# First two experts' second-layer weights split during the attention, by VectorE and GpSimd, with buffers refilled in order of release

## The chip, the cores and the metric

One NeuronCore of a Trainium2 chip. The metric is the device time of one execution in microseconds (us). The kernel before took 423.86 us (median of three runs, 423.17 to 424.08).

## The reference

Causal attention of 8 batches x 12 heads over 448 positions of 64 features feeds a mixture of experts with a capacity limit. Cut to what matters:

```python
scores = np.where(mask, -1e9, scale * np.matmul(q, k.transpose(0, 1, 3, 2)))
attn = softmax(scores)                       # 8 x 12 x 448 x 448
x = np.matmul(attn, v)  ->  (3584, 768)      # heads side by side
probs = softmax(x @ w_gate)                  # 8 experts
for e in range(8):
    tok = tokens whose best expert is e; the 80 of largest gate weight are kept
    h = np.maximum(x[tok] @ w1[e], 0.0)      # 768 -> 1024
    out[tok] = gate_w[tok, None] * (h @ w2[e])   # 1024 -> 768
```

All inputs and the output are float32. `w1[e]` is 768 x 1024 and `w2[e]` is 1024 x 768; the two take 6.3 MB for each expert and are read once.

## The kernel before

The kernel has two stages. In the attention (about the first 275 us) a loop runs over 48 pairs of heads, six pairs (`pr.p` 0 to 5) for each of the eight batches (`bt.b`). The work of one pair is laid out by hand in eight slots (`CYCLE`, slot number `k`), and every engine executes in the order in which it is written there. TensorE computes the scores `sp` (L376), VectorE masks and scales them (`ns`, `nb`, L386, operations `m0` to `m6`, one for each tile of 64 queries), ScalarE raises them (`prob`, L393, `e0` to `e6`), TensorE transposes the previous pair's probabilities (`tp`, L411), ScalarE copies them out of PSUM (`PT`, L419, `c0` and `c1`), TensorE multiplies by the values (`xp`, L440), and VectorE copies the result (`xu`, L446). GpSimd splits the queries and keys of the pair three places ahead into two float16 parts (`split_pair`, cast L333 and two subtractions L335). Between these, steps of the routing of the batch before stand at numbered slots (`STEPS`): gate products, the ranking of the tokens, and the rows `xr` (L646) that are written to the scratch tensor `xs`. On SyncE's queue the slots 1, 4 and 7 of a pair issue one part of a weight piece each (L214), and, where no piece is under way, a store of zeros to the output.

The weights are cut into 32 pieces of 128 x 3072 float32 (1.5 MB), in the order of `PIECES`: three chunks of 128 x 1024 for a first-layer piece, four chunks of 128 x 768 for a second-layer piece. Ten buffers hold them in strict rotation: seven in `wpool`, two in `wearly` (which the attention uses for queries and keys), one more that appears at its end. Seven pieces are loaded from pair 5 on; three more follow at the end of the attention; the 22 others come through L203 as buffers come free.

In the expert stage ScalarE casts each chunk, scaled by `SW` = 32, to float16 (`wh`, L1236), and VectorE computes what the cast lost (`wl`, L1221). There are 12 `wh` and 11 `wl` slots, which TensorE frees. A split chunk costs TensorE three float16 products in the first layer (L1305, L1307, L1308) or two in the second (L1301, one of which carries both parts of the hidden values, and L1303). The function `whole` names 21 of the 112 chunks that are not split: TensorE multiplies their float32 values directly (L1293). TensorE's order is by hand here (first layer of expert e, then second layer of expert e - 1); the others are placed by the compiler's scheduler. A buffer whose chunks are all split is free when the last `wl` of it is done; one with a whole chunk is free when TensorE has read it.

Of the kernel before, what the change touches and what calls it, by code (L numbers as in the profile page):

```python
# [7 lines left out]
F32 = mybir.dt.float32  # L8
F32R = mybir.dt.float32r
F16 = mybir.dt.float16  # L10
# [23 lines left out]
EARLY = {'gp0': 16, 'gs0': 18, 'gp1': 24, 'gs1': 26, 'lp': 32, 'lg': 34, 'logit': 37, 'shifted': 38, 'chosen': 40, 'sums': 40, 'one_hot': 41, 'weight': 41, 'weighted': 42, 'columns': 42, 'parts': 43, 'r0t': 45, 'r1t': 45, 'r0c': 46, 'r1c': 46, 'c3w': 48, 'rl': 49, 'c0w': 50, 'c3l': 51, 'c0l': 52, 'lt': 53, 'c2w': 54, 'c2l': 55, 'c1w': 56, 'c1l': 57, 'cp': 58, 'ro': 59, 'places': 60, 'places_more': 61, 'gt': 62, 'own': 63, 'earlier': 64, 'rank': 65, 'rr': 66, 'rr_more': 67, 'tn': 68, 'tab': 69, 'rp': 70, 'row': 71}  # L34
ROWS_EARLY = [(0, 0, 14, 1, 1), (0, 1, 22, 1, 4), (1, 0, 30, 1, 4), (1, 1, 47, 7, 8)]
LATE = 19

TAIL = """
rest3 ta ya rest3 v0 tb yb rest3 rest rest v1 rest2 turned vy guard invert rest placed w rest2 rest gp0 wy rest5 gp1 close piece gs
# [8 lines left out]
def attention_then_moe(  # L48
# [24 lines left out]
    assert NT == 4 and LAST == QB and D == NP * P and D // 2 <= S - LAST  # L73


    const = ctx.enter_context(tc.tile_pool(name="const", bufs=1))
    keep = ctx.enter_context(tc.tile_pool(name="keep", bufs=1))
    wpool = ctx.enter_context(tc.tile_pool(name="wraw", bufs=1))
# [98 lines left out]
    WBUF, WMORE = max(2, 8 - max(1, NSL)), 3  # L177

    WEARLY = 2

    RING, WHOLE = 3, 3
    qk_raw = wearly.tile([P, PW], F32, name="qk", tag="w", bufs=WEARLY)
    qk_parts = wearly.tile([P, 2 * PW], F16, name="qk16", tag="w", bufs=WEARLY)
    wload = []
    wmore = [wearly]

    def piece():

        e, which, c, k = PIECES[len(wload)]
        x = len(wload) % (WBUF + WMORE)  # L190
        pool, bufs = (wpool, WBUF) if x < WBUF else (wmore[0], WEARLY) if x < WBUF + WEARLY else (wmore[1], WMORE - WEARLY)
        t = pool.tile([P, k, PW // k], F32, name="wraw", tag="w", bufs=bufs)
        wload.append(t)
        return t, (w1 if which == 1 else w2)[e, :, c:c + k, :]

# [9 lines left out]
    def piece_parts():  # L205
# [8 lines left out]
            nc.sync.dma_start(t[:, j, x * half:(x + 1) * half], src[:, j, x * half:(x + 1) * half])  # L214
        return [lambda j=j, x=x: part(j, x) for j in range(k) for x in range(2)]


    mv = one_hots = mv_flat = oh_flat = expert_cols = tables = table_rows = None
    identb = before = dec = number = number_after = pnum = tbase = wgd = slots_e = slots_t = None
# [826 lines left out]
    with tc.manual_schedule():  # L1046
# [20 lines left out]
        for i, pr in enumerate(pairs):  # L1067
            bt = pr.bt
            if pr.p == 0:
                bt.xu = spool.tile([P, NP, S], F32, name="xu", tag="xu")  # L1070
                bt.sums = spool.tile([P, NP * TILES], F32, name="sums", tag="sums", bufs=3)
                if bt.b < B - 1:
                    batch_plan(bt)
            pr.xu, pr.sums = bt.xu, bt.sums
            if i and i % PH == 0:
                load_values(i // PH)
            products, masked, raised = scores_groups(pr, i)
            ops = {"s0": lambda: products(0), "s1": lambda: products(1)}
            for t in range(TILES):
                ops[f"m{t}"], ops[f"e{t}"] = lambda t=t: masked(t), lambda t=t: raised(t)  # L1080
            if i:
                for x, (work, copy) in enumerate(transpose_groups(pairs[i - 1], i < APART)):
                    ops[f"t{x}"], ops[f"c{x}"] = work, copy
            if i >= 2:
                values.append(values_group(pairs[i - 2]))
                ops["v"], ops["xu"] = values[-1]
            for k in range(SLOTS):
                for name in CYCLE[k].split():
                    if name in ops:
                        ops.pop(name)()  # L1090
                for f in plan.pop(i * SLOTS + k, []):
                    f()

                if i < WHOLE and k == 4:
                    load_pair(i + RING)
                if i >= WHOLE - 1 and k == (5 if i < WHOLE else 0) and i + RING + 1 < n:
                    load_pair(i + RING + 1)
                if k == 5 and pr.p == NP - 1 and i + 2 < n:
                    split_pair(i + 2)
                    split_pair(i + 3)  # L1100
                if k == 6 and pr.p < NP - 2 and WHOLE <= i + 3 < n:
                    if i >= 2:
                        nc.gpsimd.tensor_copy(tie, pairs[i - 2].xu[:, pairs[i - 2].p, 0:1])
                    split_pair(i + 3)

                if i == n - 2 and k == 0 and len(wload) >= WBUF and not parts:
                    load_piece()

                if i > 4 and k in (1, 4, 7):
                    if not parts and len(wload) < WBUF:  # L1110
                        parts = piece_parts()
                    if parts:
                        parts.pop(0)()
                    elif zdone[0] < N:
                        zero_rows()
        for f in parts:
            f()
        while len(wload) < WBUF:
            load_piece()
        while len(wload) < WBUF + WEARLY:  # L1120
# [76 lines left out]
    def whole(e, which, c):  # L1197

        if e >= E - 2:
            return e == E - 1 and which == 2 and c >= NC2 - 1  # L1200
        return c >= NC2 - 2 if which == 2 else c >= (NC1 // 2 if e == 0 else NC1 - 1)

    SW, SX = 32.0, 8.0
    NF = F // P
    HALF = NF // 2

# [6 lines left out]
    def split_pieces(m):  # L1213

        first = done[0]
        done[0] += m
        order, lows = [], []

        def low(l, src, h):
            with tc.issue_after((low_after or last_of)[-1].ins):  # L1220
                return nc.vector.scalar_tensor_tensor(out=l, in0=src, scalar=SW, in1=h, op0=ALU.mult, op1=ALU.subtract)  # L1221

        for i in range(first, first + m):
            while len(wload) <= i:
                load_piece()
            e, which, c, k = PIECES[i]
            for j in range(k):
                src = wload[i][:, j, :]
                order.append(c + j)
                if whole(e, which, c + j):  # L1230
                    parts_of[(e, which, c + j)] = (src,)
                    continue
                h = wsplit.tile([P, PW // k], F16, name="wh", tag="wh", bufs=HIS, padded_shape=[P, max(F, D)])
                l = wsplit.tile([P, PW // k], F16, name="wl", tag="wl", bufs=LOS, padded_shape=[P, max(F, D)])
                with tc.issue_after(batches[-1].raised.ins):
                    nc.scalar.activation(h, src, AF.Copy, scale=SW)  # L1236
                lows.append((l, lambda l=l, src=src, h=h: low(l, src, h)))
                parts_of[(e, which, c + j)] = (h, l)
        return order, lows

    def split_now(m):
        order, lows = split_pieces(m)
        for _, f in lows:
            f()
        return order
# [155 lines left out]
    for s in range(NSL):  # L1401
        if s:
            done[0] = 0
            wload.clear()
        units = []
        for e in range(E):
            u = Unit()
            u.e, u.s = e, s
            units.append(u)
        n1, n2 = NC1 // K1, NC2 // K2  # L1410
        prev = None
        g = gather(units[0])
        token_weights[s]()
        while s == 0 and len(wload) < WBUF + WMORE:
            load_piece(g)

        with tc.manual_schedule(engines={mybir.EngineType.PE}):
            for e in range(E + 1):
                if e < E:
                    u = units[e]  # L1420
                    if e == 0:

                        order, lows = split_pieces(n1)
                        u.order = order[NC1 // 2:] + order[:NC1 // 2]
                        units[1].order, more = split_pieces(n1)
                        for nx in units[1:AHEAD]:
                            gather(nx)
                        for _, f in lows:
                            low_after.append(f())
                        inputs(u)  # L1430
                        low_after.append(u.xl)
                        for _, f in more:
                            f()
                    elif e > 1:
                        u.order = split_now(n1)
                    if e + AHEAD < E:
                        gather(units[e + AHEAD])

                    def between(p=prev, nx=units[e + 1] if e + 1 < E else None):
                        if p and p.e:  # L1440
                            outputs(units[p.e - 1])
                        elif nx and not p:
                            inputs(nx)
                    if prev:
                        hidden(prev)
                    layer1(u, between)
                if prev:
                    prev.order = split_now(n2)
                    if e == E:
                        hidden(prev)  # L1450

                    between = None
                    if e + 1 < E:
                        between = lambda u=units[e + 1]: inputs(u)
                    elif e == E and prev.e:
                        between = lambda u=units[prev.e - 1]: outputs(u)
                    layer2(prev, between)
                    if e == E:
                        outputs(prev)
                prev = units[e] if e < E else None  # L1460
# [37 lines left out]
```

## Time and profile before

| | us |
|---|---|
| median of three runs | 423.86 |
| the profiled execution | 424.38 |
| its span, first to last instruction | 422.7 |
| TensorE busy | 399.8 (95%) |
| ScalarE busy | 370.7 (88%) |
| VectorE busy | 349.3 (83%) |
| GpSimd busy | 221.6 (52%) |
| DMA, mean over the span | 261 GB/s |

The shares are means over two stages with different limits, so the rows further on are taken by stretch. A matmul's duration on the page is that of a pipelined instruction; the pace of TensorE is read from the starts of the first instructions of successive groups. An idle time in brackets is that of the engine just before the row, with what ended it.

### The profile page before, as it was taken

The numbers are of one execution on the slowest core, as the hardware profiler recorded it, in microseconds if no ns is written. First come the engines' busy times: TensorE is split into PE (matmuls) and PEld (weight loads), VectorE is DVE, ScalarE is ACT, GpSimd is POOL, SyncE is SP. The second block draws the span as 40 slices with busy tenths as digits, with TensorE's granted clock in tenths as the row PEclk, the third lists the DMA queues.
The fourth block names the chain that finished last, engine by engine and source line by source line (L and its number), as shares of the span: only waits on it lengthen the run. The fifth ranks groups of instructions, "written<-read, shape, count | busy, mean of one in ns | idle before, by whom it ended". The sixth has DMA issues, their size and how long they took to land. (4 is left out here: it accounts for less than half of the span.)

```text
span 422.7 us, 19609 instructions
## 1 busy us (share of the span) xinstructions
PE 399.8 (95%) x7982; PEld 341.1 (81%) x7983; DVE 349.3 (83%) x1226; ACT 370.7 (88%) x980; POOL 221.6 (52%) x388
## 2 busy tenths in 40 slices
PE   5999999999999999999999999988999999999993
PEld 2688788787788878888878887875599999999993
DVE  3677688788978879888888897777789999998991
ACT  4999999999999999999999998874879898897790
POOL 3698546765845963865684586515511255230002
PEclk9999999999999999999999999999999999999998
DMA  6569977987898697798697443564489999999911
GB/s 204 155 208 323 293 266 222 339 272 241 268 329 262 223 304 251 243 272 288 204 288 259 150 145 118 206 197 190 117 302 395 380 417 396 390 422 426 383 35 47
DMA packets 42106, 110.18 MB, mean 261 GB/s; under 512 B 5234, under 2 KB 29554, under 8 KB 38816
## 3 DMA queue, kind: packets, MB, share of 16 engines
q1 hardware_dynamic: 40816, 105.20, 71.6%
q0 software_dynamic: 1056, 3.51, 2.6%
q8 instruction: 62, 1.02, 1.0%
q14 instruction: 28, 0.23, 0.2%
q10 hardware_dynamic: 144, 0.23, 0.2%
HBM read 85.35 MB, written 23.99 MB: 259 GB/s over the span
## 5 line engine op out<-in xcount | busy, mean ns | idle before, releaser
L393 ACT ACTIVATE prob<-ns,nb 128x448 f32<-128x448 f32 (+6 forms) x336 | 167.9, 503 | 15.3 <-DVE nb L386 14.5
L386 DVE CUSTOM_DVE_ANT_0 ns<-sp,mask 128x448 f32<-128x448 f32 (+6 forms) x336 | 124.9, 418 | 40.5 <-PE sp L376 33.5
L440 PE MATMUL xp<-PT,vt 128*64 128x128 f32 (+3 forms) x1536 | 95.8, 277 | 0.3 <-issue 0.3
L1221 DVE SCALAR_TENSOR_TENSOR wl<-wraw,wh 128x768 f16<-128x768 f32 (+1 forms) x91 | 92.1, 1077 | 3.0 <-ACT wh L1236 2.9
L335 POOL TENSOR_TENSOR qk<-qk,qk 128x448 f16<-128x448 f32 x90 | 91.9, 1043 | 3.6
L419 ACT COPY PT<-tp 128x1024 f32<-128x1024 f32 x89 | 89.0, 1000 | 3.0 <-PE tp L411 2.6
L440 PEld LDWEIGHTS xp<-PT,vt 128*64 128x64 f32 x1536 | 80.1, 137 | 13.7 <-issue 1.0
L376 PE MATMUL sp<-qk 64*64 64x384 f16 (+8 forms) x1974 | 79.2, 283 | 4.7 <-DMA qk<-k_t 4.7
L1236 ACT ACTIVATE wh<-wraw 128x768 f16<-128x768 f32 (+1 forms) x91 | 79.1, 932 | 3.5 <-PE hp L1308 1.5
L411 PE MATMUL tp<-ident,prob 64*128 64x64 f32 x1424 | 63.3, 227 | 6.0 <-ACT PT L419 4.2
L411 PEld LDWEIGHTS tp<-ident,prob 64*128 64x128 f32 x1424 | 51.9, 139 | 16.6 <-ACT PT L419 8.3
L393 ACT ACTIVATION_READ_ACCUMULATOR prob<-ns,nb 128x1 f32 x336 | 64.3, 191 | 0.0
L376 PEld LDWEIGHTS <-qk 64*64 64x64 f16 x1890 | 50.9, 106 | 12.7
L1394 POOL DMA_INDIRECT out<-yo,idx x8 | 19.7, 2466 | 66.0 <-ACT yo L1391 61.8
L333 POOL CAST qk<-qk 128x896 f16<-128x896 f32 x45 | 42.0, 933 | 8.5 <-DMA qk<-k_t 8.4
L1308 PEld LDWEIGHTS <-wl 128*128 128x128 f16 x362 | 36.1, 100 | 1.4 <-DVE wl L1221 1.2
L1305 PEld LDWEIGHTS <-wh 128*128 128x128 f16 x362 | 36.4, 101 | 0.9 <-issue 0.9
L1307 PEld LDWEIGHTS <-wh 128*128 128x128 f16 x362 | 36.2, 100 | 0.0
L1305 PE MATMUL hp<-xh,wh 128*128 128x80 f16 x320 | 35.3, 202 | 0.8 <-issue 0.8
L1308 PE MATMUL hp<-xh,wl 128*128 128x80 f16 x320 | 35.3, 202 | 0.0
L1307 PE MATMUL hp<-xl,wh 128*128 128x80 f16 x320 | 35.3, 202 | 0.0
L446 DVE COPY xu<-xp 128x448 f32<-128x448 f32 x48 | 29.7, 619 | 5.5 <-PE xp L440 5.1
(193 smaller groups left out, 633.1 us busy)
## 6 DMA issues: line engine op xcount, KB each, us to landing
wraw<-w SPq DMA_DIRECT2D x25, 1536.0 KB, 13.8
qk<-q_t SPq DMA_DIRECT2D x48, 224.0 KB, 3.9
out<-mask SPq DMA_DIRECT2D x56, 192.0 KB, 4.0
qk<-k_t SPq DMA_DIRECT2D x47, 224.0 KB, 4.3
vt<-v_t SPq DMA_DIRECT2D x16, 576.0 KB, 6.1
wraw<-w SPq DMA_DIRECT2D x30, 256.0 KB, 5.2
xs<-xr SPq DMA_DIRECT2D x18, 384.0 KB, 4.3
wraw<-w SPq DMA_DIRECT2D x16, 192.0 KB, 4.4
```

The lines of the kernel that those rows point to most:

```text
L335: nc.gpsimd.tensor_tensor(out=l[:, part], in0=x[:, part], in1=h[:, part], op=ALU.subtract)
L376: nc.tensor.matmul(pr.sp[t][to], q[rows, t * QB:(t + 1) * QB], k[rows, 0:WIDTH[t]], start=(x == 0), stop=(x == len(terms) - 1), skip_group ...
L386: nc.vector.tensor_tensor_reduce(out=ns[:, 0:w], in0=pr.sp[t], in1=mask[:, S - w:S], scale=-1.0 / 8.0, scalar=HUGE, op0=ALU.add, op1=ALU.m ...
L393: nc.scalar.activation(pr.P[:, OFF[t]:OFF[t] + w], ns[:, 0:w], AF.Exp, bias=nb, scale=-1.0, accum_out=pr.sums[:, pr.p * TILES + t:pr.p * T ...
L411: nc.tensor.transpose(tp[r][:, at:at + QB], pr.P[rows, off:off + P], ident[rows, rows])
L419: (nc.scalar.copy if how == "a" else nc.vector.tensor_copy)(pr.PT[:, g], pr.tp)
L440: nc.tensor.matmul(xp[rows, x0 * QB:x1 * QB], st["vt"][:, c, p * P + j * DH:p * P + (j + 1) * DH], pr.PT[:, g, 1 - j if crossed else j, at ...
L1221: return nc.vector.scalar_tensor_tensor(out=l, in0=src, scalar=SW, in1=h, op0=ALU.mult, op1=ALU.subtract)
L1236: nc.scalar.activation(h, src, AF.Copy, scale=SW)
L1305: nc.tensor.matmul(o, wh[:, ws], ah[:, c, :], start=(x == 0 and i % per == 0), stop=False, skip_group_check=True)
L1307: nc.tensor.matmul(o, wh[:, ws], al[:, c, :], start=False, stop=False, skip_group_check=True)
L1308: nc.tensor.matmul(o, wl[:, ws], ah[:, c, :], start=False, stop=(x == n - 1), skip_group_check=True)
```

## The change

Six things change. (1) The four second-layer pieces of experts 0 and 1 come first in `PIECES`. They are loaded during the attention into `w4`, `w5`, `w6` and `w4` again, at pairs fixed by `LOADS`. (2) Their 16 chunks are split during the attention: VectorE multiplies a chunk in place by 32 (16 instructions), GpSimd casts it to float16 (16) and subtracts the cast from it in two halves (32). The table `PRESPLIT` places them by pair and slot: one scaling each in slots (1, 7), (2, 7) and (4, 1), three casts in (4, 4), three subtractions each in (1, 3) and (2, 3); scalings and casts in batches 1 to 6, subtractions in batches 2 to 7. (3) The halves stay in four buffers, `w0` to `w3`, each of the size of a raw piece. (4) The other pieces go to buffers in the order of `FIRST` and `NEXT_USE` instead of the strict rotation. (5) `whole` names 13 chunks instead of 21: the two last second-layer chunks of experts 0 and 1 are among those split ahead, and the last first-layer chunk of experts 1 to 4 is split in the expert stage. (6) In that stage the second layers of experts 0 and 1 are neither cast nor subtracted any more.

```diff
+LOADS = [5, 7, 9, 25, 31, 37, 45]
+PRESPLIT = {(1, 3): (0, 0, 3), (1, 7): (1, 0, 0), (2, 3): (0, 0, 3), (2, 7): (1, 0, 0), (4, 1): (1, 0, 0), (4, 4): (0, 3, 0)}
...
+    PRE = 4 if WBUF == 7 and E > 1 and NC2 == 2 * K2 else 0
+    FIRST = [f"w{x}" for x in range(WBUF)] + ["e"] * WEARLY + ["m"] * (WMORE - WEARLY)
+    NEXT_USE = list(FIRST)
+    if PRE:
+
+        PIECES = [x for x in PIECES if x[0] < 2 and x[1] == 2] + [x for x in PIECES if x[0] > 1 or x[1] == 1]
+        FIRST = ["w4", "w5", "w6", "w4", "w5", "w6", "w4", "e", "e", "m"]
+        NEXT_USE = ["w5", "w4", "w6", "e", "e", "w0", "w1", "m", "w2", "w3"]
...
+    whalves = [wpool.tile([P, K2, 2, D], F16, name="wpre", tag=f"w{x}", bufs=1) for x in range(PRE)]
...
-        e, which, c, k = PIECES[len(wload)]
-        x = len(wload) % (WBUF + WMORE)
-        pool, bufs = (wpool, WBUF) if x < WBUF else (wmore[0], WEARLY) if x < WBUF + WEARLY else (wmore[1], WMORE - WEARLY)
-        t = pool.tile([P, k, PW // k], F32, name="wraw", tag="w", bufs=bufs)
+        i = len(wload)
+        e, which, c, k = PIECES[i]
+        x = FIRST[i] if i < len(FIRST) else NEXT_USE[i % len(FIRST)]
+        pool, bufs = {"e": (wearly, WEARLY), "m": (wmore[-1], WMORE - WEARLY)}.get(x, (wpool, 1))
+        t = pool.tile([P, k, PW // k], F32, name="wraw", tag=x if pool is wpool else "w", bufs=bufs)
...
+    presplits = [], [], []
+
+    def presplit(i):
+
+        for j in range(K2):
+            h, l = (whalves[i][:, j, x] for x in range(2))
+            src = wload[i][:, j, :]
+            presplits[0].append(lambda src=src: nc.vector.tensor_scalar(src, src, SW, None, op0=ALU.mult))
+            presplits[1].append(lambda src=src, h=h: nc.gpsimd.tensor_copy(h, src))
+            for x in (slice(0, D // 2), slice(D // 2, D)):
+                presplits[2].append(lambda src=src, h=h, l=l, x=x: nc.gpsimd.tensor_tensor(
+                    out=l[:, x], in0=src[:, x], in1=h[:, x], op=ALU.subtract))
...
+                for x, todo in zip(PRESPLIT.get((pr.p, k), ()), presplits):
+                    for f in todo[:x] if 0 < bt.b - (todo is presplits[2]) < B - 1 else []:
+                        f()
+                        todo.remove(f)
+
                 if i > 4 and k in (1, 4, 7):
-                    if not parts and len(wload) < WBUF:
+                    if not parts and len(wload) < WBUF and (not PRE or i >= LOADS[len(wload)]):
                         parts = piece_parts()
+                        if len(wload) <= PRE:
+                            presplit(len(wload) - 1)
...
-        return c >= NC2 - 2 if which == 2 else c >= (NC1 // 2 if e == 0 else NC1 - 1)
+        if which == 2:
+            return e >= PRE // 2 and c >= NC2 - 2
+        return c >= (NC1 // 2 if e == 0 else NC1 - 1) and (e == 0 or e == E - 3)
...
+                if i < PRE:
+                    parts_of[(e, which, c + j)] = tuple(whalves[i][:, j, x] for x in range(2))
+                    continue
...
+                        seconds = [split_pieces(n2)[0] for _ in range(PRE // 2)]
...
-                    prev.order = split_now(n2)
+                    prev.order = seconds.pop(0) if seconds else split_now(n2)
```

## Rows read from the trace of the kernel before

**Rows 1.** By stretch: length, busy (instructions) of PE, PEld, DVE, ACT, POOL; clock; DMA
```profile
180.00:240.00 60.00, 59.17 (x1312) 49.00 (x1310) 51.62 (x241) 57.71 (x174) 36.48 (x67) 1.00 0.80 255
310.00:320.00 10.00, 9.20 (x210) 9.07 (x210) 9.03 (x12) 7.13 (x12) 1.15 (x1) 1.00 0.91 296
370.00:380.00 10.00, 10.00 (x205) 10.00 (x205) 10.00 (x13) 9.17 (x15) 3.73 (x1) 1.00 1.01 424
400.00:410.00 10.00, 9.85 (x208) 9.43 (x204) 9.12 (x13) 9.41 (x17) 0.92 (x1) 1.00 0.19 64
```

**Rows 2.** Groups by shape: xcount | busy us, mean ns | idle before
```profile
L1236 ACT ACTIVATE wh<-wraw 128x768 f16<-128x768 f32 x51 | 39.9, 840 | 1.7 <-PE op L1301 0.7 <-PE op L1303 0.7 <-ACT hh L1325 0.2
L1221 DVE SCALAR_TENSOR_TENSOR wl<-wraw,wh 128x1024 f16<-128x1024 f32 x40 | 46.5, 1228 | 1.4 <-ACT wh L1236 1.4
L1221 DVE SCALAR_TENSOR_TENSOR wl<-wraw,wh 128x768 f16<-128x768 f32 x51 | 46.1, 959 | 1.5 <-ACT wh L1236 1.5
L335 POOL TENSOR_TENSOR qk<-qk,qk 128x448 f16<-128x448 f32 x90 | 91.9, 1043 | 3.6
L333 POOL CAST qk<-qk 128x896 f16<-128x896 f32 x45 | 42.0, 933 | 8.5 <-DMA qk<-k_t 8.4
```

**Rows 3.** The chain that ended last, by time: start us, us, what
```profile
375.13 1.75 PE hp L1293 x16
...
379.83 0.07 PE op L1301
...
381.10 2.71 PE op L1293 x24
383.81 0.04 PE hp L1305
...
388.11 0.66 PE ytp L1387 x6
```

**Rows 4.** Timeline, the last piece's chunks: start us, us, engine, instruction
```profile
408.58 2.32 ACT L1236 ACTIVATE wh<-wraw 128x768 f16<-128x768 f32 x3
410.48 2.69 DVE L1221 SCALAR_TENSOR_TENSOR wl<-wraw,wh 128x768 f16<-128x768 f32 x3
```

**Rows 5.** Timeline, first slots of a pair p = 4 and start of the next
```profile
197.25 0.55 DVE L386 CUSTOM_DVE_ANT_0 ns<-sp,mask 128x384 f32<-128x384 f32 x1
197.37 0.67 ACT L393 ACTIVATE prob<-ns,nb 128x448 f32<-128x448 f32 x1 [0.45 <-DVE nb L386]
198.04 0.60 ACT L393 ACTIVATE prob<-ns,nb 128x384 f32<-128x384 f32 x1
202.80 0.71 PE L411 MATMUL tp<-ident,prob 64*128 64x64 f32 x16 [0.33 <-ACT PT L419]
196.96 2.04 POOL L335 TENSOR_TENSOR qk<-qk,qk 128x448 f16<-128x448 f32 x2
```

**Rows 6.** Timeline, first mask of the pairs p = 2 and p = 3, and first exponential
```profile
184.38 0.62 DVE L386 CUSTOM_DVE_ANT_0 ns<-sp,mask 128x448 f32<-128x448 f32 x1
190.51 0.62 DVE L386 CUSTOM_DVE_ANT_0 ns<-sp,mask 128x448 f32<-128x448 f32 x1 [0.68 <-PE sp L376]
185.04 0.67 ACT L393 ACTIVATE prob<-ns,nb 128x448 f32<-128x448 f32 x1
```

**Rows 7.** Lines 735 and 479 (ns min/median/max), and timeline beside the extremes
```profile
L735 DVE CAST oh<-goh x1: 204/204/204, 292.6 to 292.6; 128x96 bf16<-128x96 f32 x1
292.90 0.20 DVE L710 TENSOR_TENSOR gow<-goh,ggw 128x32 f32<-128x32 f32 x1
L479 POOL COPY norm<-sums x60: 185/195/492, 37.5 to 286.0; 64x12 f32<-64x12 f32 x45, 64x6 f32<-64x6 f32 x15
284.73 0.90 DVE L849 TENSOR_TENSOR rm<-ro,slots_e 80x320 bf16<-80x320 f16 x2
284.79 0.90 POOL L479 COPY norm<-sums 64x12 f32<-64x12 f32 x2 [8.56 <-DVE ro L829]
```

**Rows 8.** Timeline, VectorE in a later slot of that pair p = 4
```profile
200.43 0.55 DVE L912 TENSOR_TENSOR rr<-rank,slots_t 128x160 bf16<-128x160 f16 x2
```

More of the change, by code (lines that the diff above doesn't have):

```diff
@@ L73, in attention_then_moe @@
     assert NT == 4 and LAST == QB and D == NP * P and D // 2 <= S - LAST
+    SW, SX = 32.0, 8.0
     const = ctx.enter_context(tc.tile_pool(name="const", bufs=1))
@@ L1117, in attention_then_moe @@
             f()
+        for todo in presplits:
+            for f in todo:
+                f()
         while len(wload) < WBUF:
@@ L1200, in whole @@
             return e == E - 1 and which == 2 and c >= NC2 - 1
-        return c >= NC2 - 2 if which == 2 else c >= (NC1 // 2 if e == 0 else NC1 - 1)
-    SW, SX = 32.0, 8.0
+        if which == 2:
+            return e >= PRE // 2 and c >= NC2 - 2
+        return c >= (NC1 // 2 if e == 0 else NC1 - 1) and (e == 0 or e == E - 3)
     NF = F // P
```

## The prediction, on record before the result

> **What bounds the kernel now.** I read the table by stretch first, since the page's mean shares mix two stages [rows 1]. In the attention (180 to 240 us) TensorE is busy 59.17 of 60 us and ScalarE 57.71: both are full, VectorE has 8.4 us of slack in 60, GpSimd 23.5. In the expert stage (370 to 380 us) TensorE, VectorE and the DMA are all full and ScalarE nearly (9.17 of 10). From 400 us the DMA is done (share 0.19) and the tail runs through the last chunks' casts and subtractions.
>
> The pace of one chunk on TensorE comes from starts in the chain [rows 3]. A whole first-layer chunk takes 1.75 us. Five split ones stand between 383.81 and 388.11, 0.86 us each. Two whole second-layer chunks take 2.71 us, 1.355 each; the two split ones before them stand between 379.83 and 381.10, 0.635 each.
>
> In the attention the question is which delay reaches TensorE. At the end of a pair p = 4 it waited 0.33 us for ScalarE's copy `PT` [rows 5]. From 197.37 to that copy ScalarE has no gap, and what it waited for at 197.37 was VectorE's first mask. So there a delay of VectorE reaches the end one for one, less the little that its result lies ready before ScalarE takes it.
>
> **The change part by part.** *Expert stage, TensorE.* Eight chunks change from whole to split: four of the first layer at 1.75 - 0.86 = 0.89 and four of the second at 1.355 - 0.635 = 0.72, together -6.4 us [rows 3].
>
> *Expert stage, VectorE.* Twelve subtractions of 768 go (the other four of the 16 chunks were whole), at 46.1/51 = 0.90 us of engine time; four of 1024 come, at 46.5/40 = 1.16 [rows 2]: -10.8 + 4.7 = -6.2 us. *ScalarE:* twelve casts at 39.9/51 = 0.78 go, four a third longer (estimate 1.04) come: -5.2 us, on the engine that has a little slack. Three engines that were level all lose 5 to 6.4 us, so none of them takes the place of another.
>
> *Expert stage, DMA.* The bytes are the same, and so is what is in the buffers at its start: four pieces as halves and six raw, where ten were raw. So 22 pieces still have to come through a full queue. It can only start sooner: in 310 to 320 us it moved 296 GB/s against 424 later [rows 1]; with buffers taken in the order of their release (the first-layer pieces of experts 1 and 2, all split now, free at their last subtraction) at most (424 - 296) x 10 us = 1.3 MB, some 3 us, comes forward. The stream ends near 402 us (0.19 x 10 us after 400), and the last piece's casts began at 408.58 [rows 4]: 6.5 us of slack. The engines' 6 us fit in that, but hardly more. Pieces in the middle have less slack than the last, which the rows don't show one by one; so I take -5.5 us, with -3.5 and -6.4 as ends.
>
> *Attention, VectorE's scalings.* No row has this instruction, in place over 768 float32 values. Upper end: a subtraction of the same 768 columns, 0.90 us of engine time [rows 2]. Its two shapes, 959 ns for 768 and 1228 for 1024, are 0.15 us and 1.05 ns a value. Lower end: twice that pace. The trace has one instruction from one input in SBUF to SBUF, a cast of 96 float32 values in 204 ns [rows 7]; at 1.05 ns a value it would be 0.25 us, at half that 0.20. So a scaling is 0.15 + 768 x 0.525 ns = 0.55 us by the cast, some 0.5 of engine time (neighbours overlap by 0.06). I take 0.5, since the cast is the nearest in kind. [...]
>
> What of it lies on the path: (2, 7) stands before a gap of 0.68 us in which VectorE waits for TensorE [rows 6], and is hidden by it. (1, 7) has no gap: the first mask of the next pair moves by 0.5 us, and so does ScalarE's exponential at 185.04 (its mask ended at 185.0). One pair later ScalarE waited 0.45 us, as at 197.37 [rows 5], so that is taken up before TensorE needs it. (4, 1) stands between the masks of 448 and 384 columns. The latter ended at 197.80 and ScalarE took it at 198.04: 0.24 us of cover, so 0.26 us, say 0.3, reaches TensorE at 202.80. Scalings at (4, 1) are in five batches: 1.5 us. For what the (1, 7) ones leave over, and small waits for GpSimd, I add 0.1 a batch: +2.0 us, from 1.5 to 4 (at 0.9 us a scaling: 0.7 at (4, 1), 0.1 at the others, five times).
>
> *Attention, GpSimd.* 16 casts at 933 x 768/896 = 0.80 us and 32 subtractions at 1043 x 384/448 = 0.89 us [rows 2]: 41 us over six batches, some 208 us, 0.20 of it on top of 36.48/60 = 0.61 [rows 1]. What hides them is GpSimd's idle time; behind them wait the query and key splits, needed two pairs later (12 us, by the 6.1 us between two first masks in [rows 6]), while 2.7 us is what a slot puts before them. If that cover went, scores would wait. Cost 0.
>
> *Loads and the queue.* The pieces in the attention are the same seven, five of them later; 255 GB/s in 180 to 240 us [rows 1] leaves room. A load waits on SyncE's queue for its buffer only if the subtractions of the piece before are late; by the table they are done four pairs ahead at least, except the last (pair 43, two pairs ahead). Behind it would wait the row stores. Cost 0.
>
> *Sum.* 424.38 (profiled) - 5.5 + 2.0 = 420.9. The profiled execution is 0.5 us above the median of the runs, so the median should be **420.4 us**. About 0.2% is what a measurement of this kernel can tell from no change.
>
> **The rivals.** *1. VectorE waits for GpSimd (slower).* The trace shows one direction: a copy of GpSimd that takes 195 ns took 492 beside a VectorE instruction with two inputs in SBUF [rows 7]: it waited for it. If a scaling that reads at two values per cycle in turn waits for a running GpSimd instruction, the place is again (4, 1): at 197.3 GpSimd is in the first of two subtractions from 196.96 to 199.00 [rows 5], so the scaling starts at about 198.0, 0.7 us later, and 1.0 us a batch reaches TensorE instead of 0.3. At (1, 7) the new subtractions run; half of one is 0.45 us more, of which 0.25 passes. At 200.43 two more instructions with two inputs in SBUF [rows 8] would wait for the new casts, which follow the subtractions there, some 0.5 us. That is 1.8 us a batch, 9 us in five: 424.4 - 5.5 + 9 - 0.5 = 427.4 us. It decides once the loss in a batch is over 1.1 us. For it: the row of 492 ns, and that GpSimd is four fifths busy then. Against: nothing in the trace shows VectorE as the one that waits; its masks and copies run beside GpSimd at their usual length, but they have one input in SBUF. [...] Chance 0.27.
>
> *2. Scalings at one value per cycle, or half of rival 1.* Cost 4 to 5.5 us instead of 2.0: 422.4 to 424, say 423. For: the nearest row by shape is the 0.90 us one. Chance 0.15.
>
> *3. The experts' gain is hidden.* The stream is late in the middle (one piece late by 3 us), and the engines wait for it where they no longer wait for each other: 424.4 - 3 + 2 - 0.5 = 422.9. For: the DMA is full from 320 on. Against: the slack of 6.5 us at the end. Chance 0.08.
>
> **How the numbers follow.** The forecast as it stands has 0.50, with its own range of 417.5 to 422.5. Faster by over 0.2% (under 423.0): 0.50, half of rival 2 (0.08) and a little of rival 3 (0.03): 0.61. Within 0.2%: 0.07 + 0.05, and 0.02 of rival 1: 0.14. Slower: 0.25. The range that should hold it 8 times in 10 reaches from the forecast's best (gain 6.4, price 1.5, and a stream 2 us sooner in the tail: 417) to rival 1's 427.
>
> **What would show it.** In the changed profile: 83 casts `wh` and 83 `wl` (91 now); whole first-layer products in experts 0 and 5 alone; the time from the first expert's product to the end shorter by about 5.5 us. The scalings' mean: about 0.56 us says the price holds, 0.96 rival 2, and 1 us or more with wide spread rival 1. TensorE's waits for ScalarE's copies after a pair p = 4: 0.6 us each for the forecast, 1.3 for rival 1. The first product of the expert stage: 2 us later by the forecast, 9 us by rival 1. What would make the sum wrong outright: scores that wait for late splits, or a weight load that holds SyncE's queue.

## The result, and the profile after

The changed kernel takes 427.88 us (median of 427.16 to 428.98) against 423.59 for the one before: a ratio of 1.0105, 95% interval 1.0089 to 1.0121. It is slower; the forecast was 420.4, faster, in a range that ended at 427.

The profiled execution took 428.53 us, its span is 426.6 (before: 424.38 and 422.7). The line of the float32 first-layer product splits the span in two; the first row is of the kernel before, the second of the one after (count, ns min/median/max, first and last start):

```profile
L1293 PE MATMUL hp<-xw,wraw x48: 275/275/337, 306.6 to 311.9; 128*128 128x80 f32 x48
L1333 PE MATMUL hp<-xw,wraw x48: 274/276/338, 313.0 to 318.3; 128*128 128x80 f32 x48
```

The first expert product comes 6.4 us later (forecast: 2.0), and from it to the end of the span it takes 113.6 us instead of 116.1: 2.5 less (forecast: 5.5). Both steps failed, and both to the same side.

**The attention.** Groups of the kernel after, from 40 to 268 us (count | busy us, mean ns | idle before):

```profile
L238 DVE TENSOR_SCALAR wraw<-wraw 128x768 f32<-128x768 f32 x16 | 14.7, 919 | 0.0
L938 DVE TENSOR_TENSOR rr<-rank,slots_t 128x160 bf16<-128x160 f16 x10 | 5.9, 626 | 0.0
L875 DVE TENSOR_TENSOR rm<-ro,slots_e 80x320 bf16<-80x320 f16 x8 | 5.3, 697 | 0.0
L241 POOL TENSOR_TENSOR wpre<-wraw,wpre 128x384 f16<-128x384 f32 x32 | 31.5, 1013 | 0.0
```

The 16 scalings (L238) take 919 ns, not 550. Two comparisons that were there before, with both inputs in SBUF, have grown as well: L875 (L849 before) from 482 to 697 ns, L938 (L912, [rows 8]) from 313 to 626. The timeline answers [rows 8] (start us, us); the last two rows are of an earlier slot (1, 7):

```profile
202.03 0.61 DVE L238 TENSOR_SCALAR wraw<-wraw 128x768 f32<-128x768 f32 x1
202.30 2.23 POOL L361 TENSOR_TENSOR qk<-qk,qk 128x448 f16<-128x448 f32 x2
205.18 2.55 POOL L239 CAST wpre<-wraw 128x768 f16<-128x768 f32 x3
205.72 1.33 DVE L938 TENSOR_TENSOR rr<-rank,slots_t 128x160 bf16<-128x160 f16 x2
...
187.56 2.98 POOL L241 TENSOR_TENSOR wpre<-wraw,wpre 128x384 f16<-128x384 f32 x3
188.59 1.17 DVE L238 TENSOR_SCALAR wraw<-wraw 128x768 f32<-128x768 f32 x1
```

The pair of comparisons that took 0.55 us takes 1.33 under the new casts, and the two subtractions beside the scaling 2.23 us where [rows 5] has 2.04. That scaling, at (4, 1), took only 0.61 us: the new subtractions had pushed GpSimd's old one behind its start. The one at (1, 7) took 1.17 us beside a new subtraction. The five scalings at (4, 1) took 604 to 945 ns, the six at (1, 7) 847 to 1205. No column names this as a wait: the idle time before each is 0.0. It shows only as an instruction that is longer than its kind.

**The expert stage.** By stretch, as in [rows 1]; the first two rows are of the kernel before:

```profile
320.00:330.00 10.00, 10.00 (x158) 10.00 (x155) 9.16 (x12) 8.29 (x15) 1.66 (x1) 1.00 1.02 423
330.00:340.00 10.00, 10.00 (x199) 10.00 (x196) 10.00 (x11) 9.50 (x15) 3.99 (x1) 1.00 1.00 376
...
320.00:330.00 10.00, 8.49 (x221) 8.36 (x219) 9.00 (x11) 6.73 (x9) 0.41 (x1) 1.00 0.97 362
330.00:340.00 10.00, 8.02 (x137) 7.72 (x135) 7.53 (x10) 5.55 (x9) 0.96 (x1) 0.83 1.01 387
370.00:380.00 10.00, 10.00 (x192) 10.00 (x190) 10.00 (x15) 9.06 (x15) 1.60 (x1) 1.00 1.01 423
```

From 320 to 340 TensorE is busy 16.5 us of 20 (before: all 20), and its clock falls; from 370 to 380 three engines are full as before. The timeline of ScalarE, and then of TensorE, says why:

```profile
331.44 1.06 ACT L1276 ACTIVATE wh<-wraw 128x1024 f16<-128x1024 f32 x1 [2.98 <-DMA wraw<-w]
334.62 0.56 ACT L1318 ACTIVATE xh<-xtp 128x480 f16<-128x480 f32 x1
335.23 0.20 PE L1345 MATMUL hp<-xh,wh 128*128 128x80 f16 x1 [1.10 <-ACT xh L1318]
336.24 0.23 PE L1347 MATMUL hp<-xl,wh 128*128 128x80 f16 x1 [0.81 <-DVE xl L1319]
```

ScalarE stands 2.98 us at a cast whose load has not landed. The next input's high part (`xh`) waits in its queue behind that cast, and TensorE for it.

### The profile page after: what moved, and what is told of

It is laid out like the page before. It is cut to its first block, busy times and chain, and to the rows that moved or that the text cites. A ratio compares the mean times of both kernels' runs of the same rounds, so it can differ in the third digit from the quotient of the medians.

```text
span 426.6 us, 19725 instructions
## 1 busy us (share of the span) xinstructions
PE 397.5 (93%) x8014; PEld 337.3 (79%) x8015; DVE 360.2 (84%) x1234; ACT 361.9 (85%) x966; POOL 256.4 (60%) x436
## 5 line engine op out<-in xcount | busy, mean ns | idle before, releaser
L361 POOL TENSOR_TENSOR qk<-qk,qk 128x448 f16<-128x448 f32 x90 | 93.5, 1059 | 3.6
L1258 DVE SCALAR_TENSOR_TENSOR wl<-wraw,wh 128x1024 f16<-128x1024 f32 (+1 forms) x83 | 86.0, 1095 | 1.9 <-ACT wh L1276 1.7
L402 PE MATMUL sp<-qk 64*64 64x384 f16 (+8 forms) x1974 | 80.4, 283 | 4.7 <-DMA qk<-k_t 4.6
L1276 ACT ACTIVATE wh<-wraw 128x1024 f16<-128x1024 f32 (+1 forms) x83 | 74.3, 953 | 8.8 <-DMA wraw<-w 4.4
L1434 POOL DMA_INDIRECT out<-yo,idx x8 | 14.3, 1790 | 73.1 <-ACT yo L1431 68.9
L1345 PE MATMUL hp<-xh,wh 128*128 128x80 f16 x352 | 40.7, 205 | 2.6 <-issue 1.5
L1345 PEld LDWEIGHTS <-wh 128*128 128x128 f16 x394 | 40.3, 102 | 1.6 <-issue 1.6
L1347 PE MATMUL hp<-xl,wh 128*128 128x80 f16 x352 | 40.7, 205 | 0.8 <-DVE xl L1319 0.8
L1348 PEld LDWEIGHTS <-wl 128*128 128x128 f16 x394 | 40.0, 102 | 1.6 <-issue 0.9
L1347 PEld LDWEIGHTS <-wh 128*128 128x128 f16 x394 | 40.1, 102 | 1.4 <-issue 1.2
L1348 PE MATMUL hp<-xh,wl 128*128 128x80 f16 x352 | 40.7, 205 | 0.0
```

The source lines that it names most:

```text
L361: nc.gpsimd.tensor_tensor(out=l[:, part], in0=x[:, part], in1=h[:, part], op=ALU.subtract)
L402: nc.tensor.matmul(pr.sp[t][to], q[rows, t * QB:(t + 1) * QB], k[rows, 0:WIDTH[t]], start=(x == 0), stop=(x == len(terms) - 1), skip_group ...
L1345: nc.tensor.matmul(o, wh[:, ws], ah[:, c, :], start=(x == 0 and i % per == 0), stop=False, skip_group_check=True)
L1347: nc.tensor.matmul(o, wh[:, ws], al[:, c, :], start=False, stop=False, skip_group_check=True)
L1348: nc.tensor.matmul(o, wl[:, ws], ah[:, c, :], start=False, stop=(x == n - 1), skip_group_check=True)
```

## The experiments: the attention

In the sketches `-` is the changed kernel.

**No scalings.**

```diff
-presplits[0].append(lambda src=src: nc.vector.tensor_scalar(src, src, SW, None, op0=ALU.mult))
+presplits[0].append(lambda: None)
```

> The 16 VectorE scalings of the first two experts' second layers are left out; GpSimd's casts and subtractions stay. Theory A (VectorE's instructions that read two operands of SBUF and GpSimd's wait for each other, whoever added them): the two comparisons of the gathered rows at L875 and L938 stay long (means near 620 ns, single ones near 1.1 us, against 483 and 313 before), and only what the scalings themselves delay comes back: 2 to 3 us of the attention's 6.4, so about 425.3. Theory B (the scalings' own time in VectorE's queue is the loss): all 6.4 come back, about 421.5, and the comparisons are back at their former durations.

423.98 us, ratio to the kernel before 1.0011 (0.9998 to 1.0024). The first product comes at 308.9: 4.1 us come back, more than the 2 to 3 of theory A and not the 6.4 of B (0.3 of them already in the first batch, where neither kernel has a scaling, so that part is what two executions differ by). The comparisons stay long, and GpSimd's subtractions are back at one length:

```profile
L938 DVE TENSOR_TENSOR rr<-rank,slots_t 128x160 bf16<-128x160 f16 x10 | 6.7, 712 | 0.0
L875 DVE TENSOR_TENSOR rm<-ro,slots_e 80x320 bf16<-80x320 f16 x8 | 5.3, 697 | 0.0
L241 POOL TENSOR_TENSOR wpre<-wraw,wpre 128x384 f16<-128x384 f32 x32 | 28.5, 919 | 0.0
```

So the loss has two parts: about 4 us by the scalings, and 2.3 that GpSimd's new work costs without them. That the comparisons are the second part is argued so far; the run with the new places tests it.

**Scalings that keep a running sum.**

```diff
-nc.vector.tensor_scalar(src, src, SW, None, op0=ALU.mult)
+nc.vector.tensor_scalar(src, src, SW, None, op0=ALU.mult, op1=ALU.add, accum_out=scaled)
```

> The scalings are made in another form, with a running sum kept beside, which should read one value per cycle (near 0.95 us each, as other instructions with such a sum do) and not share GpSimd's access. Theory A: all 16 take the same time, 0.95 to 1.05 us, whatever GpSimd does, and GpSimd's own subtractions beside them are no longer stretched; the comparisons at L875 and L938 stay long; since the mean of the scalings was 0.92 us already, the time stays within 1 us of 427.9. Theory B (VectorE's queue time alone): the same mean, but single scalings still between 0.55 and 1.34 us.

427.60 us, 1.0096 (1.0058 to 1.0133), first product at 312.1. All 16 take 941 to 954 ns (946 on average), also here, where a GpSimd subtraction runs, and that is not stretched either (three in 2.68 us, against 2.98 beside a scaling of the changed kernel):

```profile
187.12 2.68 POOL L243 TENSOR_TENSOR wpre<-wraw,wpre 128x384 f16<-128x384 f32 x3
188.12 0.95 DVE L239 TENSOR_SCALAR_CACHE_REDUCE wraw<-wraw 128x768 f32<-128x768 f32 x1
```

Theory A holds: beside GpSimd's instructions the scalings without the sum took 549 to 1339 ns, those with it 941 to 954, and as the waits had brought the former to 0.92 us on average, little is won: the first product comes 0.9 us sooner, 0.3 of it before the first scaling, and the medians are 0.3 us apart.

**Scalings alone.** GpSimd's casts and subtractions are left out. In a first version the zeros for the halves were written at the start, which held GpSimd's first splits up by 10 us (438.01 us); its first product says nothing, but its scalings were as long, 0.55 to 1.42 us.

> The scalings stay; GpSimd's 16 casts and 32 subtractions of the weights are left out (the halves are filled with zeros at the start, so the first two experts give zeros). Theory A: the scalings take 0.55 us each except beside GpSimd's older work, the comparisons are back near 483 and 313 ns, and about 4.5 of the attention's 6.4 us come back: first expert product near 308.5, the run near 423.4. Theory B (the scalings' own time is the loss): the first product stays near 312.5 and the run near 427.5.

The second version writes them in 16 pieces:

```diff
+if 1 <= i <= 8 and k in (4, 7):
+    x = 2 * (i - 1) + (k == 7)
+    nc.gpsimd.memset(whalves[x // 4][:, x % 4], 0.0)
```

> As the run without GpSimd's casts and subtractions, but the zeros that take the place of the halves are written in small pieces in the first two batches, so that the start of the kernel isn't delayed by them. The scalings then meet only GpSimd's older work. By the prediction's own step (0.5 us of engine time, 2 us in all over the attention) the first product comes at 308.6 us, and the run is near 423.5. If a scaling costs its time wherever it stands (16 x 0.5), the first product is at 310 to 312 and the run at 425 to 427.

The zeros still cost 8 us in the second batch, so neither the first product (319.0) nor the time (433.92) can be compared. The batches behind can. First masks of pair 12 and of pair 42, before and here:

```profile
69.12 0.62 DVE L386 CUSTOM_DVE_ANT_0 ns<-sp,mask 128x448 f32<-128x448 f32 x1 [0.64 <-PE sp L376]
242.75 0.62 DVE L386 CUSTOM_DVE_ANT_0 ns<-sp,mask 128x448 f32<-128x448 f32 x1 [0.72 <-PE sp L376]
...
77.22 0.62 DVE L410 CUSTOM_DVE_ANT_0 ns<-sp,mask 128x448 f32<-128x448 f32 x1 [0.67 <-PE sp L400]
255.12 0.62 DVE L410 CUSTOM_DVE_ANT_0 ns<-sp,mask 128x448 f32<-128x448 f32 x1 [0.72 <-PE sp L400]
```

173.63 us became 177.90: 13 scalings cost 4.3 us with no new GpSimd work at all, at a granted clock of 1.00. (The first version lost 6.4 us between the same masks, but there the clock fell in two batches, to 0.69 from 144 to 148 and from 184 to 188 us.) Where the prediction looked, at (4, 1):

```profile
207.87 2.36 POOL L359 TENSOR_TENSOR qk<-qk,qk 128x448 f16<-128x448 f32 x2
207.91 1.42 DVE L238 TENSOR_SCALAR wraw<-wraw 128x768 f32<-128x768 f32 x1
209.84 0.62 ACT L417 ACTIVATE prob<-ns,nb 128x384 f32<-128x384 f32 x1 [1.05 <-DVE nb L410]
...
194.96 0.56 DVE L238 TENSOR_SCALAR wraw<-wraw 128x768 f32<-128x768 f32 x1
194.97 1.34 POOL L357 CAST qk<-qk 128x896 f16<-128x896 f32 x1
```

At 207.91 the scaling started 0.04 us after a subtraction of the query split, which was there before the change and takes 1.04 us by itself. The scaling took 1.42 us, so by its length it waited for that one's end; ScalarE waited 1.05 us for the mask behind it. At 194.96 the scaling was first by 0.01 us: it took 0.56 and the cast 1.34 instead of 0.93. In both cases it was the one that started second that took longer than its kind. With GpSimd's old work in its old place, these 13 scalings are even longer than the same 13 in the changed kernel, 960 ns on average against 899.

**GpSimd's work at other places.** First the fold: no scalings, and the outputs of the first two experts multiplied by 32 more, so that the result is the reference's, and the load order of the next section.

```diff
-nc.scalar.activation(to, t[:, :, 1], AF.Copy, scale=1.0 / (SW * SW * SX))
+back = 1.0 / (SW * SX) if u.e < PRE // 2 else 1.0 / (SW * SW * SX)
+nc.scalar.activation(to, t[:, :, 1], AF.Copy, scale=back)
...
```

> No scalings, as in the run that left them out, but the factor of 32 that the first two experts' weights now lack is given back at their outputs, so that the result is the reference's; and the two loads in the order of the load-order run. If the two effects are separate, the first product comes at 308.9 us (the scalings cost 4.1 us of the attention) and the stage behind it is 1.2 to 1.5 us shorter than without the new load order: near 422.7. If the pauses of TensorE in the expert stage come from VectorE's queue and not from that load, the stage stays as it was: 424.0.

423.55 us, 1.0003 (0.9987 to 1.0019); first product at 308.7, the stage behind it 0.5 us shorter than without the load order, not 1.2 to 1.5. Then the places, with a copy ahead of the first cast that makes GpSimd wait for the comparison:

```diff
-PRESPLIT = {(1, 3): (0, 0, 3), ..., (2, 3): (0, 0, 3), ..., (4, 4): (0, 3, 0)}
+PRESPLIT = {(1, 3): (0, 0, 2), ..., (2, 3): (0, 0, 2), ..., (3, 3): (0, 0, 1), ..., (4, 6): (0, 1, 0), (5, 1): (0, 2, 1)}
...
+if (pr.p, k) == (4, 6) and 0 < bt.b < B - 1 and presplits[1] and compared:
+    nc.gpsimd.tensor_copy(tie, compared[-1])
```

> The run before this one, with GpSimd's casts and subtractions put at other places: two subtractions at (1,3), two at (2,3), one at (3,3), a cast at (4,6) behind the second comparison at L938, two casts and a subtraction at (5,1). By theory A (VectorE's two-operand comparisons wait for GpSimd) L875 and L938 go back to about 0.48 and 0.31 us, the first product comes at 306.8 us as in the kernel before, and the run is near 420.6. By a rival (GpSimd's own work is late because of what is added, the query and key splits above all), the first product stays near 308.9 or is later, and the run stays near 422.7.

421.46 us, **0.9958 (0.9942 to 0.9973): faster than both kernels.** The comparisons are back at 481 and 310 ns, and the first product at the time of the kernel before:

```profile
L876 DVE TENSOR_TENSOR rm<-ro,slots_e 80x320 bf16<-80x320 f16 x8 | 3.5, 481 | 0.0
L940 DVE TENSOR_TENSOR rr<-rank,slots_t 128x160 bf16<-128x160 f16 x10 | 2.7, 310 | 0.0
L1337 PE MATMUL hp<-xw,wraw x48: 275/275/337, 306.6 to 311.9; 128*128 128x80 f32 x48
```

GpSimd does the same 48 instructions. It had the time for them, as the prediction said; what they cost was VectorE's. From the first mask of pair 6 to that of pair 42, which leaves out what executions differ by before, it took 207.6 us in the kernel before, 213.8 in the changed one, 210.1 without scalings and 208.0 here. So the new places give back 2.1 us, and 0.5 are left.

The waits aren't all gone, either. Two other instructions with both inputs in SBUF, 179 and 182 ns on average before, now meet a cast and a subtraction in four batches:

```profile
L706 DVE SCALAR_TENSOR_TENSOR goh<-gsh,dec 128x32 f32<-128x32 f32 x6 | 3.1, 514 | 0.0
L717 DVE TENSOR_TENSOR goh<-goh,gfm 128x32 f32<-128x32 f32 x6 | 2.6, 438 | 0.0
```

Together they grew by 3.5 us (6 x 335 and 6 x 256 ns), and with only 0.5 us left in all, little of that reaches the path: where a wait falls decides what it costs.

**The new places, with the scalings kept.** (The places of the run above in the changed kernel.)

> The changed kernel with VectorE's scalings and its load order as they are; only GpSimd's casts and subtractions stand at the other places. If the two causes in the attention add up, the 2.1 us of the comparisons come back and the 4.1 us of the scalings stay: first product at 310.9 us, the run near 425.8. If the scalings, now beside other GpSimd work, lengthen or shorten with what runs at their start, the first product is off from that: 309.5 if they meet short remainders, 312 if they meet whole subtractions.

428.16 us, 1.0121 (1.0096 to 1.0146), first product at 312.1: the dearest case of the expectation. The comparisons are short (487 and 309 ns), but the scalings now meet other remainders, 926 ns on average; one of 1351 ns at (4, 1) stands in a batch that took 37.8 us instead of 35.2. Half of that is TensorE's clock, which fell right behind that scaling (by stretch, as in [rows 1]):

```profile
134.00:138.00 4.00, 2.87 (x67) 2.38 (x63) 3.93 (x15) 3.78 (x11) 3.56 (x6) 0.94 1.07 336
138.00:142.00 4.00, 4.00 (x64) 3.43 (x64) 2.82 (x14) 2.74 (x12) 3.55 (x12) 0.64 0.51 172
```

The pair in which it fell took 1.4 us longer than before. Without that, by estimate, the first product would stand at 310.7 us, close to the 310.9 of two costs that add up. So the run doesn't decide whether they do.

## The experiments: the expert stage

**The load order.**

```diff
-with tc.manual_schedule(engines={mybir.EngineType.PE}):
+with tc.manual_schedule(engines={mybir.EngineType.PE, mybir.EngineType.SP}):
```

> Only the order of two loads in SyncE's queue is changed: the second half of the fourth expert's first layer goes ahead of the first half of the third expert's second layer, which is the order in which they are used. Theory (the refills stand in the wrong order, and ScalarE's casts behind the late one hold TensorE): that load is issued at about 317.4 us, when the subtractions of its buffer end, and no longer at 319.04; it lands about 4 us sooner than 331.34, TensorE's pauses at 326.85, 335.23 and 336.24 (1.5, 1.1 and 0.8 us) go for the most part, and the run is about 3 us shorter, near 425. Rival (the stream as a whole is late, whatever its order): the pauses only move, and the time stays within 0.5 us of 427.9. On either, the first expert product stays at 313.0 us.

SyncE's loads now stand in the order in which the kernel writes them. 426.73 us, 1.0080 (1.0055 to 1.0105), so 1.2 us less than the changed kernel. The load was issued at 317.10 and landed at 323.61 (319.04 and 331.34 in the changed kernel). ScalarE no longer waits for it:

```profile
324.77 3.89 ACT L1276 ACTIVATE wh<-wraw 128x1024 f16<-128x1024 f32 x4
330.18 0.57 ACT L1318 ACTIVATE xh<-xtp 128x480 f16<-128x480 f32 x1
```

TensorE's pauses (the waits of TensorE in the stage) went from 1.5, 1.1 and 0.8 us to 1.5, 0.6 and 0.5: the longest is now for VectorE's `xl`. The order was a cause, of less than half of the expected 3 us. Not all of that is pauses: in the traces the stage is 1.4 us shorter, 0.7 by its pauses and 0.7 by TensorE's own work, and the clock that had fallen in the changed kernel (0.57 from 336 to 340 us) stays full here (1.00 from 312 to 400).

**One part undone.** The last first-layer chunk of four experts whole again:

```diff
-return c >= (NC1 // 2 if e == 0 else NC1 - 1) and (e == 0 or e == E - 3)
+return c >= (NC1 // 2 if e == 0 else NC1 - 1)
```

> One part of the change is undone: the last chunk of the first layer of four experts (not the first, not the sixth) is used whole again, in float32, as before. TensorE gets 4 x 0.89 = 3.6 us more, VectorE 4 x 1.16 less, ScalarE 4 x 1.04 less. If TensorE bounds the stage, as the prediction has it, the run is 3 to 3.6 us longer: 431. If the pauses for loads, casts and subtractions bound it, they shrink by as much as TensorE gains work: within 1.5 us of 427.9. The attention is the same: first product at 313.0.

429.39 us, 1.0138 (1.0110 to 1.0166): by medians 1.5 us more than the changed kernel, which is the bound of the second theory and half of the first. The trace is of the slowest of its five executions (431.40): there TensorE's own work in the stage rose by 4.0 us (3.6 expected) and its pauses fell by 0.8. So TensorE does get the work; how much of it reaches the run is 1.5 us by medians and 3 by the two profiled executions, and part of it is lost in pauses.

**The input first.** Added to the run with the new places:

```diff
+if e == 3:
+    low_after.append(units[2].xl)
 u.order = split_now(n1)
```

> The run with GpSimd's work at other places, and one more edit: VectorE takes the low part of the third expert's input (the instruction at the line of xl) ahead of the fourth expert's weight subtractions, two of which stood before it. In the run without this edit its operand was ready at 324.6 us, VectorE came to it at 327.33, and TensorE waited 1.34 us for it. Theory (the order in VectorE's queue costs that pause): the pause goes, the expert stage is 1 to 1.3 us shorter, the run near 420.3. Rival (VectorE is full there, with no idle time between 317 and 334 us): the two subtractions come later by as much, TensorE waits for them instead, and the time stays within 0.4 us of 421.5.

421.83 us, 0.9957 (0.9939 to 0.9975): no gain that can be measured. VectorE in the run without the edit:

```profile
317.45 6.89 DVE L1262 SCALAR_TENSOR_TENSOR wl<-wraw,wh 128x1024 f16<-128x1024 f32 x6
324.26 0.88 DVE L1370 SCALAR_TENSOR_TENSOR hh<-hp,hh 128x320 f16<-128x320 f32 x2
325.06 2.34 DVE L1262 SCALAR_TENSOR_TENSOR wl<-wraw,wh 128x1024 f16<-128x1024 f32 x2
327.33 0.65 DVE L1323 SCALAR_TENSOR_TENSOR xl<-xtp,xh 128x480 f16<-128x480 f32 x1
```

With it, `xl` stands at 325.27 and TensorE's pause at 328.0 is gone, but the one at 332.6 grew from 0.54 to 1.49 us. By medians the rival holds: VectorE is full there, and a pause that is taken away comes back behind it.

**One more half.**

```diff
-HIS, LOS = 12, 11
+HIS, LOS = 13, 11
```

> The run with the third expert's input first, with one buffer more for the high halves of the split weights (13 for 12). There ScalarE's casts stop at 309.8 us for want of a free one, go on at 314.2 when TensorE releases the first, and VectorE, without weights to subtract, is idle for 1.8 us from 314.9; from 317 on it is full. Theory (the number of halves keeps casts and subtractions from running ahead, and so the expert stage from its gain): one cast and one subtraction come some 4 us sooner, VectorE's later work 1 to 1.2 us sooner, TensorE's pauses near 332 and 345 us shrink by about that, and the run is near 420.8. Rival (another limit stands right behind it: TensorE's order, or the loads): within 0.4 us of 421.8.

423.30 us, 0.9989 (0.9972 to 1.0005): by medians 1.5 us slower than without, where theory and rival had a gain and nothing. ScalarE and VectorE without the edit (first three rows) and with it:

```profile
307.06 2.96 ACT L1280 ACTIVATE wh<-wraw 128x1024 f16<-128x1024 f32 x3
312.82 0.57 ACT L1322 ACTIVATE xh<-xtp 128x480 f16<-128x480 f32 x1 [2.80 <-PE xtp L1315]
316.86 0.89 DVE L1370 SCALAR_TENSOR_TENSOR hh<-hp,hh 128x320 f16<-128x320 f32 x2 [1.79 <-ACT hh L1369]
...
308.92 3.91 ACT L1280 ACTIVATE wh<-wraw 128x1024 f16<-128x1024 f32 x4
315.79 0.57 ACT L1322 ACTIVATE xh<-xtp 128x480 f16<-128x480 f32 x1 [2.96 <-PE xtp L1315]
319.04 0.89 DVE L1370 SCALAR_TENSOR_TENSOR hh<-hp,hh 128x320 f16<-128x320 f32 x2 [2.00 <-ACT hh L1369]
```

The first half of the theory came true: with a buffer free ScalarE makes a fourth cast ahead of `xh`. The second fell: the subtraction of that cast stands behind the hidden values (`hh`) in VectorE's queue, and VectorE is idle before them as it was. Against the first product, `xh` itself comes 1.1 us later in this execution; TensorE's transposes waited 0.92 us for the gathered input. Why the run is not even level stays open; its profiled execution, the slowest of the twelve, also lost 1.9 us in the first batch, far from the edit.

## Why the prediction was wrong, step by step

- **The scaling's price: right alone, wrong in company.** The 0.55 us holds where no wait is in it (550 and 549 ns at 158.20 and 194.49 us of the changed kernel); the step took it for all 16 and put the wait for GpSimd into a rival. Measured: 0.92 us on average, about 4 us on the path instead of 2.0. The prediction's own upper end, 4 us at 0.9 us a scaling, has this size by luck: it stood for a scaling that is slow by itself. Rival 1 was right that VectorE waits for GpSimd. Its place (4, 1), beside an old subtraction, shows in the run without GpSimd's new work (1.42 us); in the changed kernel the long scalings stand at its second place, (1, 7), beside the new subtractions. Its size was too large: 9 us in five batches, measured 6.4 in all. What the prediction calls one and two values per cycle are its paces of 1.05 and 0.525 ns a value, and the "about 0.56 us" of its test is the 0.55 by the cast; no run shows a cycle.
- **"Against: nothing in the trace shows VectorE as the one that waits."** This is the argument that failed. Before the change, from 40 to 268 us, no VectorE instruction with both inputs in SBUF started while one of GpSimd's ran: the comparisons of [rows 8] fell into a gap of GpSimd. That a row is missing was no evidence. The row of 492 ns [rows 7] had one direction. The runs show both: 1.42 us for the scaling that started second and 0.56 for the one that started first, with the cast beside that one at 1.34 instead of 0.93; 626 ns instead of 313 for the comparison, which has two inputs in SBUF; and 941 to 954 ns for all 16 with the running sum, beside GpSimd's subtractions too.
- **GpSimd at cost 0: failed, though its cover held.** Neither splits nor scores were late. The cost was on VectorE's old comparisons: 2.1 us come back in the run with the new places, where they are short again. Rival 1 had seen those at L912 (0.5 us in each of five batches) and not those at L849, which an old subtraction reached because the new ones had pushed it back.
- **TensorE's term (-6.4): right, but for the clock.** From the first expert product to the last matmul, TensorE's time less its pauses was 108.6 us before and 102.3 to 102.8 in the five runs with the new expert stage and a full clock (load order, no scalings, fold, new places, input first); in the changed kernel, where the clock fell, 103.5. VectorE's sum fell by 6.7 us (forecast 6.2), ScalarE's by 7.8 (5.2).
- **"Three engines that were level all lose, so none takes the place of another": failed.** It compares sums over 110 us. Pauses are 4.1 us in all against 1.6 before, and the new ones stand in the first 25 us. There one late load (2.98 us ahead of ScalarE's cast at 331.44, with `xh` behind it), or the hidden values (1.79 us ahead of VectorE's `hh` at 316.86 in the run with the input first), holds what TensorE needs next.
- **The DMA stream, "up to 3 us sooner": failed.** The refills did not go by the release of their buffers, as the title has it. A load that had to wait for TensorE's read until 318.6 stood ahead of one whose buffer was free at 317.3; the second refill came 5.6 us after the first product in both kernels. This is rival 3's mechanism, a piece in the middle late by its 3 us or more, at 1.2 us for the run.
- **Sum:** +6.4 instead of +2.0 and -2.5 instead of -5.5 make 7.4 us; 420.4 + 7.4 is 427.8. The -2.5 is 5.0 us less work of TensorE (some 6 where the clock stays full) and 2.5 more pauses. Rival 1's 427.4 is near by accident: both its loss and its gain were too large.
- **Open:** what stands behind the last pauses of the expert stage (3.7 us of idle TensorE in the run with the input first). VectorE is full from 317 to 333 us, and it had idle time before that; one buffer more let ScalarE's cast start sooner, but not VectorE's subtraction. An order of VectorE's queue with that subtraction ahead of the hidden values was not tried. Whether the costs of scalings and comparisons add up is open, too.

## What to carry to other kernels

Before VectorE work is put beside GpSimd work, list every VectorE instruction of the kinds that waited here (two inputs in SBUF: 626 ns instead of 313; the scaling from one input in SBUF to SBUF: 919 on average instead of 549) with GpSimd's instruction at that moment, the old ones on both sides too. Their price here was near what was left of that instruction (0.62 us more with 0.75 left), and it appeared as length, not as a wait. An idle engine's time is free only where nothing on the path has to stand aside for it: the same 48 GpSimd instructions cost 2.1 us more at one set of places than at another, where they still lengthened two instructions, but with slack behind them. A scaling by a power of two is best not done at all if it can be folded into a factor that is applied anyway: without the scalings 4.1 us came back here.

## What the runs showed of the hardware

- Beside a running GpSimd instruction a scaling was longer by nearly what that one had left. In the changed kernel it took 604, 945 and 1169 ns with 0.19, 0.53 and 0.75 us left (129.43, 58.22 and 188.59 us), and 549 at the shortest; in the run of the scalings alone 1420 with about 1.0 us left.
- GpSimd's next instruction was longer in turn. Of the three subtractions from 187.56 us on (changed kernel) the first two took 0.91 us each. The second ended at 189.34, the scaling beside it at 189.76, and the third took 1.24.
- Where the starts are 0.01 us apart, their order doesn't tell who waits. A subtraction started 0.01 us behind the scaling at 194.49 and at 121.98 us of the changed kernel: the first time the scaling took 0.55 us and the subtraction 1.32, the second time 1.34 and 0.91.
- The running sum turned a scaling of 550 ns into one of 946, plus 83 ns to read the sum, and in exchange none of the 16 was stretched beside GpSimd (941 to 954 ns); the new subtractions took 924 ns on average, against 1013 in the changed kernel.
- TensorE's clock. After pauses that left it busy for 2.26 us of 4, the granted clock was 0.57 over the next 4 us in the changed kernel:

```profile
332.00:336.00 4.00, 2.26 (x38) 1.96 (x36) 3.14 (x4) 3.70 (x7) 0.61 (x1) 1.00 1.00 421
336.00:340.00 4.00, 3.76 (x64) 3.76 (x64) 4.00 (x6) 1.29 (x2) 0.00 (x0) 0.57 1.04 342
```

  TensorE's work was about 1 us longer there (103.5 us against 102.3 to 102.8 in the runs with a full clock), on top of the pauses. That pauses bring the clock down is not shown: in the run without scalings, nearly the same pauses (busy 2.21 of 4) were followed by a clock of 1.00:

```profile
328.00:332.00 4.00, 2.21 (x37) 1.91 (x35) 3.24 (x4) 3.60 (x7) 0.56 (x1) 1.00 0.98 415
332.00:336.00 4.00, 3.86 (x108) 3.86 (x108) 4.00 (x6) 2.78 (x4) 0.00 (x0) 1.00 1.03 335
```
